# Decay attention and a squared-ReLU MLP on one core: maxima of the unsplit heads three slots sooner, and one pair of heads divided on 64 replicated rows of sums

## The chip, the cores and the metric

The kernel runs on one core of a Trainium2 chip. The metric is the device time of one execution in microseconds (us). A profiled execution has a span, from its first to its last instruction, and a time of its own, which is a little longer. Engines are named as in the profile: PE is TensorE's matmul side and PEld its weight loads, DVE is VectorE, ACT is ScalarE, POOL is GpSimd, SP is SyncE, which issues most DMAs.

## The reference

Eight batches of eight heads, 576 positions, head dimension 64; then an MLP over the 4608 tokens.

```
def _attn_ref(q, k, v, f):
    scores = scale * np.matmul(q, k.transpose(0, 1, 3, 2))
    log_f = np.log(np.clip(f, 0.0001, 1.0))
    cum = np.cumsum(log_f, axis=-1)
    decay = cum[:, :, :, None] - cum[:, :, None, :]
    scores = np.where(causal, -1000000000.0, scores + decay)
    scores = scores - np.max(scores, axis=-1, keepdims=True)
    attn = np.exp(scores)
    attn = attn / (np.sum(attn, axis=-1, keepdims=True) + 1e-09)
    return np.matmul(attn, v)

def _moe_ref(x, w_in, w_out):
    h = np.maximum(x @ w_in, 0.0)
    return h * h @ w_out
```

The MLP takes x with all heads of a token side by side (512 wide), w_in is 512 x 2048 and w_out 2048 x 512.

## The kernel before, in words

**Slots.** The 64 heads are cut into slots, six to a head (`UNITS`): slot n = 6h + u is unit u of head h, a block of keys against the queries that may see it. The main loop goes over n from -12 to the end and writes out one slot's instructions at a time; `in_order` then keeps each engine in that order. Per slot come: the scores of (h, u) (`score`, L342 and L344, then the exponential on ACT, L361), the product of probabilities and v of two slots earlier (`av_part`, L408; `LAG` is 2), parts of the division (`finish`), the events planned for the slot's two halves with `at`, weight steps (`cv`), and MLP work (`fill`).

**Whole and split heads.** The first 14 heads (`NWHOLE`) run scores and products in full fp32 from the tile `whole[h % 2]` (named rl in the profile). The rest run as sums of rounded products, with more work on DVE and POOL. The opening, up to slot 84, is the unsplit part; there the MLP's weights are also loaded and split.

**Maxima.** The exponential needs each query's maximum first. `max_units(h)` makes six small units from a rounded copy of q and k (`rounded[h % 2]`, rk in the profile, loaded by POOL): a matmul (L309) and a reduction on DVE (L315) that writes a column of `tcol`. Each of the last reductions of the five query blocks is followed by a DMA on SP (L321) that turns the column into a piece of row 66 of the head's operand. The scores of head h read that row. For an unsplit head the units stand in slots 0, 0.5, 1, 1.5, 2, 2.5 of the head ahead (`MAXIMA`). The query blocks are done from the last to the first. Maxima have two PSUM banks in turn (`banks["m"]`: 4 and 5), scores three, until the MLP begins.

**Division.** Each v tile carries a column of ones, so that row 64 of the product is the sum of probabilities; ACT copies 64 rows to `xt` (L422) and the row of sums to `den` (L423). For each pair of heads `finish` has four parts: two DMAs spread the sums over 128 partitions as 128 x 9 (`cmp`, L433); DVE adds 1e-9 and takes reciprocals (L435, L436), and a DMA writes them to DRAM (`rdr`, L438); two DMAs broadcast them to 64 rows each (L441); POOL multiplies `xt` by them (L444). For the first batch the parts stand 2, 5, 8 and 11 slots after the pair's last slot (`DIVIDE`).

**MLP.** Tokens go in chunks of 256 over 16 blocks of the hidden layer: 16 steps a chunk, each of two halves, `mlp1` (L474, then ACT and DVE) and `mlp2` (L497) a step later. `fill` spreads the halves evenly between `ready[b-1]` and `ready[b]`, where `ready[b]` is two slots after batch b's last division: 60 for the first batch, 104 for the second. `split_x` (L461, L462) makes the MLP's rounded operand from `xt`; for the first batch it stands two slots ahead of `ready[0]`. When the first chunk's step lacks weights, the next chunk is begun, and scores then have two banks (`banks.update`).

**Weights.** 32 tiles, each in five steps: four on DVE (L189, L194, L199, L201, with a magnitude on ACT, L178, a step ahead), then a cast on ACT (L206) and a subtraction on POOL (L207). Tiles are loaded up to four ahead (L169). `RATES` says how many steps a slot takes in five stretches: n below -6, below -3, below 0, up to `ready[0]`, and after.

Of the kernel before, what the change touches and what calls it, by code (L numbers as in the profile page):

```python
# [9 lines left out]
F32 = mybir.dt.float32  # L10
# [26 lines left out]
def decay_attention_relu2_kernel(  # L37
# [18 lines left out]
    nc = tc.nc  # L56

    NH, D, _, S = qk.shape
    P = 2 * D
    H = 8  # L60
    B = NH // H
    NJ = v.shape[2]
    NT, DM = out.shape
    NF = w_in.shape[0]
    NCC = DM // P
    T = 256
# [4 lines left out]
    EPS = 1e-9  # L71
# [4 lines left out]
    NWHOLE = 14  # L76
    DEPTH = 4
    cpool = ctx.enter_context(tc.tile_pool(name="cpool", bufs=1))
    wk = ctx.enter_context(tc.tile_pool(name="wk", bufs=2))
# [5 lines left out]
    def bank(use):  # L85

        turn = banks[use] or banks["s"]
        b = turn.pop(0)
        turn.append(b)
        return psum.tile([P, 512], F32, name=f"bank{b}")  # L90
# [21 lines left out]
    whole = [wk.tile([P, 2, S], F32, name="rl") for _ in range(2)]  # L112
# [23 lines left out]
    def load_f():  # L136
        nc.sync.dma_start(out=ft, in_=f)
# [84 lines left out]
    QT = [(0, D)] + [(D + i * P, P) for i in range((S - D) // P)]  # L222
# [4 lines left out]
    NU = len(UNITS)  # L227
    state = {}
# [8 lines left out]
    def load_cum(h, k):  # L237

        if h < 2:
            nc.sync.dma_start(out=f32(k[D:D + 2, :]), in_=cum[0][h:h + 1])  # L240
        else:
            nc.sync.dma_start(out=f32(k[D:D + 2, :]), in_=cum_dr[h])
# [9 lines left out]
    def load_whole(h):  # L252
# [3 lines left out]
        if cum:  # L256
            load_cum(h, x[:, 1])

    def load_v(h):
        if h < NH:  # L260
            vr = state[h]["vr"] = wk.tile([P, NJ, D + 2], F32, name="v", bufs=3)
            nc.sync.dma_start(out=vr[:, :, :D], in_=v[h])
            if h < NWHOLE:
                nc.gpsimd.memset(vr[:, :, D:], 1.0)
# [34 lines left out]
    def max_units(h):  # L299

        st = state[h]
        tcol = wk.tile([P, 8], F32, name="tcol")

        def unit(i, k0, n, init, last):
            q0, m = QT[i]
            end = q0 + m
            ps = bank("m")
            rows = P if h < NWHOLE else D + 2
            nc.tensor.matmul(  # L309
                ps[:m, :n], st["r2"][:rows, q0:q0 + m], st["kl0"][:rows, k0:k0 + n],  # L310
                start=True, stop=True,
            )
            mo = MW - P + (k0 if m < P else max(P - end + k0, P - MW))
            acc = tcol[:m, i:i + 1] if last else tcol[:m, 7:8]
            nc.vector.tensor_tensor_reduce(  # L315
                out=ps[:m, :n], in0=ps[:m, :n], in1=mz[:m, mo:mo + n],
                op0=ALU.add, op1=ALU.min, scale=-1.0, scalar=init, accum_out=acc,
            )
            if last:
                r = st["whole"][:, 0] if h < NWHOLE else st["r2"].bitcast(F32)  # L320
                nc.sync.dma_start(out=r[D + 2:D + 3, q0:end], in_=acc)  # L321

        us = []
        for i, (q0, m) in reversed(list(enumerate(QT))):
            end = q0 + m
            if end <= 512:
                us.append(lambda i=i, end=end: unit(i, 0, end, 1e30, True))
            else:
                us.append(lambda i=i: unit(i, 0, QA, 1e30, False))
                us.append(lambda i=i, end=end: unit(i, QA, end - QA, tcol[:, 7:8], True))  # L330
        return us

    def score(h, u):
        st = state[h]
# [47 lines left out]
    def av_split(st, acc, u, o, i, first, last):  # L382
        j = UNITS[u][0]
        ph, pl = st["p"][u]
        vh, vl = st["vh"][:, j, :D + 1], st["vl"][:, j, :]
        nc.tensor.matmul(acc[:D + 1, o], vh, pl[:, i], start=first, stop=False)  # L386
        nc.tensor.matmul(acc[:D, o], vl, ph[:, i], start=False, stop=False)  # L387
        nc.tensor.matmul(acc[:D + 1, o], vh, ph[:, i], start=False, stop=last)  # L388

    def av_part(h, u, low):  # L390

        j, q0, q1 = UNITS[u]
        s0, s1 = (q0, min(q1, QA)) if low else (max(q0, QA), q1)
        if s0 >= s1:
            return
        st = state[h]
        first = u == (NU - 1 if low else 0)
        last = u == NU - 2
        if first:
            st["av"] = bank("av")  # L400
        acc = st["av"]
        base = 0 if low else QA
        o, i = slice(s0 - base, s1 - base), slice(s0 - q0, s1 - q0)
        if h < NWHOLE:

            vr = st["vr"].rearrange("p j d -> p (j d)")
            vr = vr[:, j * (D + 2):min(j * (D + 2) + P, NJ * (D + 2))]
            nc.tensor.matmul(acc[:vr.shape[1], o], vr, st["p"][u][:, i], start=first, stop=last)  # L408
        else:
            av_split(st, acc, u, o, i, first, last)  # L410
        if last:
            n = QA if low else S - QA
            if not low:
                if h % H == 0:
                    xts[h // H] = wk.tile([P, NCC, S], F32, name=f"xt{h // H % 2}", bufs=1)
                if h % 2 == 0:
                    st["den"] = wk.tile([P, S], F32, name="den")
                else:
                    st["den"] = state[h - 1]["den"]
            o = (h % 2) * D  # L420
            x = xts[h // H][o:o + D, (h % H) // 2, base:base + n]
            nc.scalar.copy(out=x, in_=acc[:D, :n])  # L422
            nc.scalar.copy(out=st["den"][o:o + 1, base:base + n], in_=acc[D:D + 1, :n])  # L423

    def finish(h, part):

        st = state[h]
        den = st["den"]
        if part == 0:
            st["cmp"] = wk.tile([P, S // D], F32, name="cmp")  # L430

            for i in range(2):
                nc.sync.dma_start(out=st["cmp"][i * D:(i + 1) * D], in_=den[i * D:i * D + 1, :])  # L433
        if part == 1:
            nc.vector.tensor_scalar_add(st["cmp"], st["cmp"], EPS)  # L435
            nc.vector.reciprocal(out=st["cmp"], in_=st["cmp"])  # L436
            st["rdr"] = dr.tile([2, S], F32, name="rdr")
            nc.sync.dma_start(out=st["rdr"].rearrange("h (p c) -> (h p) c", p=D), in_=st["cmp"])  # L438
        if part == 2:
            for i in range(2):  # L440
                nc.sync.dma_start(out=den[i * D:(i + 1) * D], in_=st["rdr"][i:i + 1].broadcast_to([D, S]))  # L441
        if part == 3:
            x = xts[h // H][:, (h % H) // 2, :]
            nc.gpsimd.tensor_tensor(out=x, in0=x, in1=den, op=ALU.mult)  # L444
            del state[h], state[h - 1]
# [98 lines left out]

    RATES = (1, 0.5, 1.5, 1.4, 2.5)
    LAG = 2
    NA = H * NU


    DIVIDE = (2, 5, 8, 11), (2, 4, 6, 7)
    MAXIMA = (0, 0.5, 1, 1.5, 2, 2.5), (1.5, 2, 2.5, 3, 3.5, 4)
    SPLIT = 0, 1, 1, 3
    LOAD = 4
    VLOAD, VSPLIT = 2, 4
# [7 lines left out]

    def fin(h, part):

        return (h + 1) * NU - 1 + DIVIDE[h >= H][part]

    avs = {}
    for n, (h, u) in enumerate(slots):  # L570
        avs.setdefault(n + LAG, []).append((h, u))
    fins = {}
    for h in range(1, NH, 2):
        for part in range(4):
            fins.setdefault(fin(h, part), []).append((h, part))
    last_slot = max(fins)
    ready = [fin(b * H + H - 1, 3) + 2 for b in range(B)]

    def fill(n, part):
# [22 lines left out]
    def cv(k):  # L602
        owed[0] += k
        convert(int(owed[0]))
        owed[0] -= int(owed[0])
# [3 lines left out]
    def at(n, half, do, *args):  # L609
        events.setdefault((n, half), []).append(lambda: do(*args))  # L610

    def max_unit(h, i):
        if i == 0:
            state[h]["max"] = max_units(h)
        state[h]["max"][i]()

    for h in range(NH):
        split = h >= NWHOLE
        if split:
            at((h - 2) * NU + LOAD, 0, load, h)  # L620
            for part in range(4):
                at((h - 1) * NU + SPLIT[part], 1, prep, h, part)
        else:
            if h > 1:
                at((h - 3) * NU + 3, 0, load_rounded, h)
                at((h - 2) * NU + 5, 1, load_whole, h)
        at((h - 1) * NU + VLOAD, 1, load_v, h)
        at((h - 1) * NU + VSPLIT, 1, split_v, h)
        for i, x in enumerate(MAXIMA[split]):
            at((h - 1) * NU + int(x), int(2 * x) % 2, max_unit, h, i)  # L630
    for b in range(B):
        at(ready[b] - 2, 0, split_x, b * S // T, b + 1)
    load_f()
    load_rounded(0)
    convert(1)
# [22 lines left out]
    for n in range(-2 * NU, last_slot + 1):  # L658
# [4 lines left out]
        if live:  # L663
            h, u = slots[n]
# [11 lines left out]
        for do in events.get((n, 0), ()):  # L676
            do()
        wr = RATES[0 if n < -NU else 1 if n < -NU // 2 else 2 if n < 0 else 3 if n < ready[0] else 4]
        cv(wr / 2)
# [50 lines left out]
```

## Time and profile before

| | |
|---|---|
| time, median of 3 runs | 1240.69 us (1238.24 to 1242.15) |
| profiled execution, its own time | 1240.77 us |
| its span | 1239.0 us |
| PE busy | 1183.2 us, 95% |
| PEld busy | 1049.6 us, 85% |
| DVE busy | 785.4 us, 63% |
| ACT busy | 701.0 us, 57% |
| POOL busy | 382.5 us, 31% |

The page's second part cuts the span into 40 equal slices and gives each engine's busy share in tenths; PEclk is the clock that TensorE was granted. A list of waits gives engine, line and tile, who was waited for, then the total in us, the number of waits and the longest. A table by stretches gives the stretch, its length, the busy us of PE, PEld, DVE, ACT and POOL with counts of instructions, the granted clock, the busy share of the DMA engines, and GB/s. A timeline gives start, duration, engine, line, operation, tiles and shapes, and in brackets the idle time before it and what ended that. Groups by shape give total busy us, mean ns, and idle time before. A wait for several semaphores is put down to the one that came last by the profile.

### The profile page before, as it was taken

What the parts mean: (1) busy time and instruction counts of PE and PEld (TensorE: products, weight loads), DVE (VectorE), ACT (ScalarE), POOL (GpSimd) and SP (SyncE); (2) the same over time, 40 slices, a digit from 0 to 9 for tenths busy, and PEclk for the clock granted to TensorE, in tenths of its full rate; (3) what the DMA queues carried; (4) which work ended last, traced back from release to release, by engine and by line L of the source; (5) the groups of instructions that cost most, each with busy time, mean ns of one, the idle gap of its engine ahead of it and who ended that gap; (6) DMA issues with size and microseconds to landing.
All of it is one profiled execution on the core that took longest, in us unless ns stands there. A gap on an engine that the chain in (4) does not pass through costs nothing.

```text
span 1239.0 us, 23289 instructions
## 1 busy us (share of the span) xinstructions
PE 1183.2 (95%) x7652; PEld 1049.6 (85%) x7652; DVE 785.4 (63%) x2044; ACT 701.0 (57%) x1720; POOL 382.5 (31%) x574
## 2 busy tenths in 40 slices
PE   3887999999999999999999999999999999999998
PEld 2555787888999899989999989998999899999997
DVE  7666677767676767666656666677676767533322
ACT  2655455566666666665565666666666666632332
POOL 3333224433333433323223233334333333200000
PEclk9989899999999999999999999999999999999999
DMA  7767640212121111121202121211121222000000
GB/s 189 172 165 179 151 125 16 53 31 58 41 58 41 48 36 49 41 58 26 58 17 53 32 58 41 52 34 47 41 58 41 58 41 58 11 28 1 18 18 17
DMA packets 115440, 71.91 MB, mean 58 GB/s; under 512 B 97244, under 2 KB 97244, under 8 KB 115320
## 3 DMA queue, kind: packets, MB, share of 16 engines
q1 hardware_dynamic: 114200, 66.30, 21.9%
q0 software_dynamic: 1120, 4.13, 1.4%
q8 instruction: 61, 1.00, 0.3%
q14 instruction: 59, 0.48, 0.1%
HBM read 60.19 MB, written 9.88 MB: 57 GB/s over the span
## 4 chain that ended last, share of the span: by engine, by line
PE 53%; ACT 2%; issue 1%; POOL 1%; DMA 1%; DVE 0%; SPq 0%; POOLq 0%; DVEq 0%; ACTq 0%
PE bank L474 21%; PE bank L497 21%; PE bank L386 2%; PE bank L351 2%; PE bank L309 2%; PE bank L388 2%; PE bank L387 2%; PE bank L348 2%; DMA den<-rdr 1%; ACT r L482 0%; ACT ph L376 0%; ACT den L423 0%; ACT p L361 0%; POOL xt L444 0%; ACT rl L277 0%
## 5 line engine op out<-in xcount | busy, mean ns | idle before, releaser
L497 PE MATMUL bank<-w,gh 128*128 128x512 f32 x1152 | 412.9, 399 | 0.0
L474 PE MATMUL bank<-xh,w 128*128 128x256 f32 x2304 | 330.7, 286 | 2.2 <-DVE tcol L315 2.1
L377 DVE TENSOR_TENSOR pl<-p,ph 128x320 fp32r<-128x320 f32 (+4 forms) x300 | 189.7, 632 | 195.3 <-ACT ph L376 187.0
L474 PEld LDWEIGHTS bank<-xh,w 128*128 128x128 f32 x2304 | 302.3, 190 | 10.2 <-DVE tcol L315 2.7
L497 PEld LDWEIGHTS bank<-w,gh 128*128 128x128 f32 x1152 | 217.1, 188 | 38.2
L482 ACT ACTIVATE r<-bank 128x256 f32<-128x256 f32 x288 | 110.6, 384 | 206.7 <-PE bank L474 193.7
L497 PE MATMUL bank<-w,gl 128*128 128x512 f32 x576 | 226.6, 393 | 0.2 <-DVE gl L485 0.2
L483 DVE TENSOR_TENSOR g<-r 128x256 f32<-128x256 f32 x288 | 127.6, 443 | 141.1 <-ACT r L482 140.3
L363 POOL TENSOR_SCALAR_AFFINE_SELECT p<-p 128x128 f32<-128x128 f32 (+1 forms) x250 | 81.6, 326 | 421.3 <-ACT p L361 267.4
L376 ACT CAST ph<-p 128x320 fp32r<-128x320 f32 (+4 forms) x300 | 124.4, 415 | 148.9 <-POOL p L363 147.1
L474 PE MATMUL bank<-xl,w 128*128 128x256 f32 x1152 | 185.5, 283 | 0.0
L474 PEld LDWEIGHTS bank<-xl,w 128*128 128x128 f32 x1152 | 158.9, 191 | 0.0
L315 DVE CUSTOM_DVE_ANT_0 bank<-bank,mz 128x256 f32<-128x256 f32 (+4 forms) x320 | 133.8, 432 | 36.6 <-PE bank L309 33.1
L361 ACT ACTIVATE p<-bank 128x320 f32<-128x320 f32 (+4 forms) x300 | 116.0, 387 | 63.9 <-PE bank L351 51.8
L485 DVE TENSOR_TENSOR gl<-g,gh 128x256 fp32r<-128x256 f32 x288 | 127.8, 444 | 36.1 <-ACT p L361 1.0
L309 PE MATMUL bank<-rk 66*128 66x320 f32 (+9 forms) x384 | 113.8, 322 | 25.1 <-DVE tcol L315 10.8
L484 ACT ACTIVATE gh<-r 128x256 fp32r<-128x256 f32 x288 | 120.5, 419 | 9.1
L497 PEld LDWEIGHTS bank<-w,gl 128*128 128x128 f32 x576 | 109.1, 189 | 14.2 <-DVE gl L485 0.9
L309 PEld LDWEIGHTS bank<-rk 66*128 66x128 f32 (+3 forms) x384 | 69.4, 186 | 43.1 <-DVE tcol L315 20.4
L386 PE MATMUL bank<-pl,vh 128*65 128x320 f32 (+4 forms) x350 | 97.1, 278 | 2.3 <-ACT den L423 2.3
L387 PE MATMUL bank<-ph,v 128*64 128x320 f32 (+4 forms) x350 | 95.0, 271 | 0.0
L388 PE MATMUL bank<-ph,vh 128*65 128x320 f32 (+4 forms) x350 | 93.3, 272 | 0.0
(75 smaller groups left out, 1515.3 us busy)
## 6 DMA issues: line engine op xcount, KB each, us to landing
qkraw<-in_qk SPq DMA_DIRECT2D x50, 288.0 KB
v<-in_v SPq DMA_DIRECT2D x64, 160.0 KB
den<-rdr SPq DMA_DIRECT2D x64, 144.0 KB
out<-osb SPq DMA_DIRECT2D x36, 256.0 KB
w<-in_w_in SPq DMA_DIRECT2D x16, 512.0 KB
w<-in_w_out SPq DMA_DIRECT2D x16, 512.0 KB
rk<-in_qk POOLq DMA_DIRECT2D x14, 288.0 KB, 4.2
rl<-in_qk SPq DMA_DIRECT2D x14, 288.0 KB
```

Source lines behind the costliest of these rows:

```text
L309: nc.tensor.matmul(ps[:m, :n], st["r2"][:rows, q0:q0 + m], st["kl0"][:rows, k0:k0 + n], start=True, stop=True,)
L315: nc.vector.tensor_tensor_reduce(out=ps[:m, :n], in0=ps[:m, :n], in1=mz[:m, mo:mo + n], op0=ALU.add, op1=ALU.min, scale=-1.0, scalar=init, ...
L376: nc.scalar.copy(out=ph[:, :n], in_=p[:, :n])
L377: nc.vector.tensor_tensor(out=pl[:, :n], in0=p[:, :n], in1=ph[:, :n].bitcast(F32), op=ALU.subtract,)
L386: nc.tensor.matmul(acc[:D + 1, o], vh, pl[:, i], start=first, stop=False)
L387: nc.tensor.matmul(acc[:D, o], vl, ph[:, i], start=False, stop=False)
L388: nc.tensor.matmul(acc[:D + 1, o], vh, ph[:, i], start=False, stop=last)
L474: nc.tensor.matmul(ph[:, :T], w[:, s, cc], x[:, cc, :], start=(cc == 0 and k == 0), stop=(cc == NCC - 1 and k == 2),)
L483: nc.vector.tensor_tensor(out=g, in0=r, in1=r, op=ALU.mult)
L484: nc.scalar.activation(out=gh, in_=r, func=AF.Square)
L485: nc.vector.tensor_tensor(out=gl, in0=g, in1=gh.bitcast(F32), op=ALU.subtract)
L497: nc.tensor.matmul(po, g[:, ts], w[:, s], start=(fc == 0 and k == 0), stop=(fc == NF - 1 and k == 2),)
```

## The change

Five things:

- The maxima of unsplit heads are planned three slots sooner, in slots -3 to -0.5 of the head ahead (`MAXIMA`). The rounded copy of q and k two heads on is loaded three slots sooner too.
- The DMAs of an unsplit head's maxima leave the units and go together, all five, in the second half of slot 0 of the head ahead (`max_rows`).
- The last pair of the first batch (heads 6 and 7, `replicated`) has 64 columns of ones beside each block of v, in tiles whose names are those of the last two weight tiles. The sums then come out on 64 partitions, ACT copies 64 rows of them to `den`, DVE adds and takes reciprocals on the whole of `den`, and POOL multiplies. There are no DMAs. The two parts stand 3 and 4 slots after the pair's last slot (`DIRECT`), so that `ready[0]` is 53.
- The first `split_x` stands one slot ahead of `ready[0]`.
- Weight steps per slot: 1 instead of 1.4 up to `ready[0]`, then 2.8 instead of 2.5.

```diff
+    def replicated(h):
+        return h // 2 == H // 2 - 1
+
     def load_v(h):
-        if h < NH:
+        if replicated(h):
+            vr = wk.tile([P, 2 * DM], F32, name=f"w{2 * NF - 1 - h % 2}", bufs=1)
+            vr = state[h]["vr"] = vr[:, :NJ * P].rearrange("p (j d) -> p j d", d=P)
+            nc.sync.dma_start(out=vr[:, :, :D], in_=v[h])
+            nc.gpsimd.memset(vr[:, :, D:], 1.0)
+        elif h < NH:
...
-            if last:
-                r = st["whole"][:, 0] if h < NWHOLE else st["r2"].bitcast(F32)
-                nc.sync.dma_start(out=r[D + 2:D + 3, q0:end], in_=acc)
+            if last and h >= NWHOLE:
+                nc.sync.dma_start(out=st["r2"].bitcast(F32)[D + 2:D + 3, q0:end], in_=acc)
...
+    def max_rows(h):
+        st = state[h]
+        r = st["whole"][D + 2:D + 3, 0]
+        for i, (q0, m) in reversed(list(enumerate(QT))):
+            nc.sync.dma_start(out=r[:, q0:q0 + m], in_=st["tcol"][:m, i:i + 1])
...
-            vr = vr[:, j * (D + 2):min(j * (D + 2) + P, NJ * (D + 2))]
+            d = st["vr"].shape[2]
+            vr = vr[:, j * d:min(j * d + P, NJ * d)]
...
-            nc.scalar.copy(out=st["den"][o:o + 1, base:base + n], in_=acc[D:D + 1, :n])
+            m = D if replicated(h) else 1
+            nc.scalar.copy(out=st["den"][o:o + m, base:base + n], in_=acc[D:D + m, :n])
...
+        if part == 1 and replicated(h):
+            nc.vector.tensor_scalar_add(den, den, EPS)
+            nc.vector.reciprocal(out=den, in_=den)
+            return
...
-    RATES = (1, 0.5, 1.5, 1.4, 2.5)
+    RATES = (1, 0.5, 1.5, 1, 2.8)
...
-    MAXIMA = (0, 0.5, 1, 1.5, 2, 2.5), (1.5, 2, 2.5, 3, 3.5, 4)
+    DIRECT = {1: 3, 3: 4}
+    MAXIMA = (-3, -2.5, -2, -1.5, -1, -0.5), (1.5, 2, 2.5, 3, 3.5, 4)
...
-        return (h + 1) * NU - 1 + DIVIDE[h >= H][part]
+        return (h + 1) * NU - 1 + (DIRECT if replicated(h) else DIVIDE[h >= H])[part]
...
-                at((h - 3) * NU + 3, 0, load_rounded, h)
+                at((h - 3) * NU, 0, load_rounded, h)
                 at((h - 2) * NU + 5, 1, load_whole, h)
+            at((h - 1) * NU, 1, max_rows, h)
...
-        at(ready[b] - 2, 0, split_x, b * S // T, b + 1)
+        at(ready[b] - 1 - (b > 0), 0, split_x, b * S // T, b + 1)
```

More of the change, by code (lines that the diff above doesn't have):

```diff
@@ L301, in max_units @@
         st = state[h]
-        tcol = wk.tile([P, 8], F32, name="tcol")
+        tcol = st["tcol"] = wk.tile([P, 8], F32, name="tcol")
         def unit(i, k0, n, init, last):
@@ L573, in decay_attention_relu2_kernel @@
     for h in range(1, NH, 2):
-        for part in range(4):
+        for part in DIRECT if replicated(h) else range(4):
             fins.setdefault(fin(h, part), []).append((h, part))
@@ L629, in decay_attention_relu2_kernel @@
         for i, x in enumerate(MAXIMA[split]):
-            at((h - 1) * NU + int(x), int(2 * x) % 2, max_unit, h, i)
+            at((h - 1) * NU + math.floor(x), int(2 * x) % 2, max_unit, h, i)
     for b in range(B):
-        at(ready[b] - 2, 0, split_x, b * S // T, b + 1)
+        at(ready[b] - 1 - (b > 0), 0, split_x, b * S // T, b + 1)
     load_f()
```

## The prediction

> **What bounds the kernel now.** I read the page's 40 slices first, then the waits of the first 130 us, then busy times by head, then the timeline around one wait, then VectorE's groups by shape.
>
> ```profile
> PE   3887999999999999999999999999999999999998
> PEclk9989899999999999999999999999999999999999
> ```
>
> A slice is 31 us. After the fourth, TensorE is the limit for the rest of the run: what the change saves must be idle or slow-clock time of TensorE in the opening. Its total work does not change (the same matmuls, in another order), so I sum losses, not work.
>
> ```profile
> PE bank L342 <- DMA rl<-tcol: 13.7, 7, 3.9
> ACT wmag L178 <- DMA w<-in_w_out: 12.9, 2, 6.9
> PE bank L342 <- DMA v<-in_v: 3.7, 1, 3.7
> ```
>
> The longest of TensorE's waits that recurs: the scores (L342) wait for rows of maxima that a DMA turns from `tcol` into the head's `whole` tile. The 3.7 us put down to v is of the same kind, as the timeline below shows.
>
> Now by head. Head h's first score is in slot 6h; each stretch runs from that matmul to the next head's. They are heads 1 to 9, then 10 and 11:
>
> ```profile
> 32.94:40.81 7.87, 7.17 (x40) 5.21 (x39) 5.71 (x18) 5.07 (x13) 2.20 (x4) 1.00 0.68 171
> 40.81:51.45 10.64, 7.63 (x41) 5.26 (x39) 7.03 (x21) 6.79 (x16) 3.58 (x6) 1.00 0.84 193
> 51.45:60.84 9.39, 7.57 (x38) 5.29 (x38) 7.21 (x19) 5.45 (x13) 3.68 (x6) 1.00 0.64 152
> 60.84:69.51 8.67, 7.36 (x37) 5.28 (x38) 5.44 (x17) 5.60 (x13) 4.18 (x6) 1.00 0.92 214
> 69.51:81.44 11.93, 7.83 (x37) 5.27 (x38) 8.56 (x23) 5.72 (x14) 4.28 (x7) 0.96 0.79 192
> 81.44:92.31 10.87, 10.26 (x38) 7.11 (x38) 6.17 (x20) 5.04 (x12) 2.56 (x5) 0.74 0.38 109
> 92.31:103.63 11.32, 7.36 (x39) 5.28 (x38) 8.02 (x21) 6.58 (x16) 4.49 (x7) 1.00 0.95 205
> 103.63:113.53 9.90, 9.20 (x37) 6.31 (x38) 6.60 (x20) 4.59 (x11) 3.12 (x5) 0.83 0.52 143
> 113.53:124.60 11.07, 7.73 (x38) 5.28 (x38) 6.29 (x18) 6.22 (x15) 3.95 (x6) 1.00 0.84 190
> 124.60:149.16 24.56, 22.44 (x116) 18.45 (x117) 16.86 (x40) 10.35 (x24) 5.79 (x7) 0.79 0.61 143
> 149.16:168.91 19.75, 19.75 (x118) 16.48 (x117) 14.85 (x34) 11.13 (x27) 5.80 (x6) 1.00 0.71 210
> ```
>
> The first number is the length, then busy PE, PEld, DVE, ACT, POOL, the granted clock, DMA share, GB/s. At clock 1.00 a head is some 7.45 us of TensorE (7.17 to 7.73). The nine heads take 91.66 us, so 91.66 - 9 x 7.45 = 24.6 us are lost. Rows account for about 15.4 (13.7 + 3.7, less 2.0 before 32.94 us). Slow clock behind waits of over 3 us accounts for some 4.6 (10.26 and 9.20 against 7.45). The other 4.6 us, 0.5 a head, are short waits.
>
> Why rows come late, at head 6:
>
> ```profile
> 76.05 0.13 DVE L315 DVE_READ_ACCUMULATOR2_ANT tcol<- 64x1 f32 x1
> 76.22 1.83 SPq L321 DMA_DIRECT2D rl<-tcol  x3
> 78.14 0.60 SPq L262 DMA_DIRECT2D v<-in_v  x1
> 78.84 0.85 SPq L321 DMA_DIRECT2D rl<-tcol  x1
> 81.44 1.41 PE L342 MATMUL bank<-rl 128*128 128x320 f32 x2 [3.65 <-DMA v<-in_v]
> ```
>
> By plan the maxima end in slot 2.5 of the head ahead. That head began at 69.51, and VectorE finished at 76.05: 6.5 us in, where 2.5 slots of 7.45/6 = 1.24 us are 3.1. Then SP issues three row requests from 76.22 to 78.05, and the score starts 3.4 us after the last of these: some 4 us of latency for the rows that the first score reads (its columns begin at 256, so it needs the first three of five).
>
> **The change, part by part.** *Maxima sooner, rows together.* Maxima are planned three slots sooner; the five requests follow in slot 0.5 of the head ahead. TensorE can be only two maxima ahead of VectorE (two banks), so VectorE is done about 1 us after slot 0; requests follow at 1.83/3 = 0.6 us each. The third leaves at 0.7 + 1.0 + 1.8 = 3.5 us, lands at 7.5, and a head without row waits lasts 7.45 + 0.5 = 7.95. So it is just in time, with 0.45 us to spare, and a busy DMA queue will still make some late. I take 0.35 us a head for that, so 8.3 us a head; ends: 0 (7.95) and 1.1 (9.05, if latency is 5.5 us). On SP, v, weight loads and the sums of the pair now stand behind five requests that wait for VectorE: weights are staged four tiles ahead, v two heads of buffers, so I cost that at nothing; if the cover fails, ScalarE waits for a tile as it did for 6.9 us in the waits above. Loading q and k three slots sooner keeps its distance to its use (nine slots); its issue on POOL and its cumulative row on SP wait for TensorE half a slot back, as before.
>
> *Rates.* From slot 0, 1 weight step a slot, not 1.4; five steps are a tile, so 1.2 tiles a head, not 1.68. Cost of a tile:
>
> ```profile
> L199 DVE SCALAR_TENSOR_TENSOR osb<-w,osb 128x512 int32<-128x512 int32 x19 | 15.1, 796 | 0.3
> L201 DVE SCALAR_TENSOR_TENSOR osb<-w,osb 128x512 int32<-128x512 int32 x19 | 13.9, 732 | 0.3
> L189 DVE TENSOR_SCALAR wmag<-wmag 128x512 f32<-128x512 f32 x20 | 13.3, 664 | 5.1 <-ACT wmag L178 5.1
> L194 DVE TENSOR_SCALAR osb<-wmag 128x512 int32<-128x512 int32 x19 | 12.0, 633 | 0.7
> L435 DVE TENSOR_SCALAR cmp<-cmp 128x9 f32<-128x9 f32 x4 | 1.4, 359 | 2.7 <-DMA cmp<-den 2.7
> L462 DVE TENSOR_TENSOR xl<-xt,xh 128x1024 fp32r<-128x1024 f32 x1 | 1.2, 1226 | 0.0
> L436 DVE RECIPROCAL cmp<-cmp 128x9 f32<-128x9 f32 x4 | 0.9, 216 | 0.1
> L461 DVE CAST xh<-xt 128x1024 fp32r<-128x1024 f32 x1 | 0.7, 695 | 4.2 <-POOL xt L444 4.2
> ```
>
> That is 0.80 + 0.73 + 0.66 + 0.63 = 2.8 us of VectorE a tile, 1.3 us a head less, and 245 KB of traffic:
>
> ```profile
> w<-in_w_in SPq DMA_DIRECT2D x12, 512.0 KB
> rk<-in_qk POOLq DMA_DIRECT2D x13, 288.0 KB, 4.2
> rl<-in_qk SPq DMA_DIRECT2D x12, 288.0 KB
> v<-in_v SPq DMA_DIRECT2D x11, 160.0 KB
> ```
>
> A head's own loads are 736 KB, so 1.35 MB a head for 1.60. VectorE's mean of the nine heads, 6.8 us, falls to some 5.4 of 8.3: neither binds here. In before, slot 60 comes 54 slots after slot 6, the nine heads; in after, the MLP may start at slot 53, 47 slots or 7.83 heads on. Loss: 7.83 x (8.3 - 7.45) = 6.7 us, where 24.6 were lost. Gain 17.9.
>
> *The opening.* Head 1's maxima now stand ahead of the first score. The fourth weight tile, for which ScalarE waits (the 6.9 us), is requested behind four more maxima, some 2 us of VectorE; TensorE has by slot 6 done about 1 us of head 2's maxima that before still owed. Net loss 1 (ends 0 and 4).
>
> *The last pair.* Sums come out of the same matmul on 64 rows. The copies cost the same:
>
> ```profile
> 34.27 0.42 ACT L422 COPY xt<-bank 64x320 f32<-64x320 f32 x1
> 34.70 0.42 ACT L423 COPY den<-bank 1x320 f32<-1x320 f32 x1
> ```
>
> Five DMAs and their latency go. In their place VectorE adds and takes reciprocals of 128x576. No row shows that. [...] I take the step from an undisturbed add of the same 9 to the reciprocal,
>
> ```profile
> 90.33 0.16 DVE L435 TENSOR_SCALAR cmp<-cmp 128x9 f32<-128x9 f32 x1
> ```
>
> which is 0.06/9 = 6.7 ns an element, so 3.9 us for 576, and 0.6 for the add and start: 4.5 us for both. [...]
>
> How the junction goes now:
>
> ```profile
> 119.69 1.27 POOL L207 TENSOR_TENSOR w<-osb,w 128x512 fp32r<-128x512 f32 x1 [4.06 <-ACT w L206]
> 119.80 1.49 DVE L194 TENSOR_SCALAR osb<-wmag 128x512 int32<-128x512 int32 x1
> ...
> 124.11 1.39 POOL L444 TENSOR_TENSOR xt<-xt,den 128x576 f32<-128x576 f32 x1 [1.75 <-DMA den<-rdr]
> ...
> 129.26 2.08 PE L474 MATMUL bank<-xh,w 128*128 128x256 f32 x8 [2.12 <-DVE tcol L315]
> ```
>
> Slot 50's division holds VectorE; head 10's maxima (slots 51 to 53.5), queued behind it, keep their banks, and TensorE stops at slot 52 for the third. After the division come POOL's product (1.39), the split of x (0.70 + 1.23) and the first MLP matmul. From the last sums at slot 49 that is 1.2 + 4.5 + 1.4 + 0.7 = 7.8 us and some 2 us of maxima and weight steps between, against four slots or 5 us of TensorE's own work: 5 us idle, and 2.5 of slow clock behind it (2.8 and 1.75 in the rows above), 7.5 in all. The same junction now loses 24.56 - 19.7 = 4.9. Net loss 2.6 (ends 0 and 12).
>
> *Slots 53 to 104.* The same 64 MLP halves are spread over 51 slots, not 44. A slot of head 11 is 19.75/6 = 3.3 us, 2.05 of that for 1.45 halves; with 1.25 halves it is 3.0. Weights cost VectorE 0.06 x 2.8 more a slot, the thinner MLP less, so its 14.85/6 = 2.5 us stay: 83% where it was 75%. Chunk 1, which leaves the scores two banks, starts near slot 71, not 80. I take 3 us for both (ends 0 and 10).
>
> Sum: 17.9 - 1 - 2.6 - 3 = 11.3 us. The profiled execution took 1240.77 us (span 1239.0), 0.08 above the median: 1229.5.
>
> **Rivals.** *More:* rows never late (loss 3.9), junction as before, opening free, VectorE no hindrance: 24.6 - 3.9 = 20.7, so 1220. For it: heads 1 and 4 run in 7.87 and 8.67 now.
>
> *Rows late anyway:* the first request leaves no sooner than before, and shorter heads ask for the same 736 KB in less time. At 9.3 us a head the loss is 14.5, and the gain 24.6 - 14.5 - 6.6 = 3.5: 1237; at 9.6, 1239.6. For it: DMA shares of 0.92 and 0.95; against: both those heads carried more weight tiles than will come.
>
> *VectorE binds from slot 53 on:* the rate of 2.8 meets a shorter slot. L194 took 1.49 us beside POOL's subtraction at 119.8, for 0.63 in the mean. If L189 and L194 were stretched so each time, by a further 0.9, VectorE would need 2.5 + 0.56 x 2 x 0.9 = 3.5 us of a 3.0 us slot for the 34 slots of weights: 17 us, less the 3 taken: 1243.5; with the larger junction, 1250. It decides against the change from 3.4 us a slot. Against it: head 11 shows 75%.
>
> **Chances.** Forecast 0.57 (1224 to 1236), more 0.16, rows late 0.17, VectorE 0.10. The range leaves out the slow case and the tail of the best: 1218 to 1240. A measurement can tell about 0.3%, 3.7 us. Faster takes the forecast nearly whole, more, and a few of rows late: 0.76; same 0.14; slower 0.10.
>
> **What would show it.** Waits of L342 for rows under 4 us in all; heads 2 to 7 at 8.0 to 8.7 us, clock near 1.00; reciprocals of 128x576 at 3.3 to 5.5 us, a gap of TensorE right behind slot 51; the first MLP matmul near 108 us, not 129.26; DVE under 90% for the 75 us after it. Wrong if heads stay above 9.3 us, if the gap is over 10, or if L474 and L497 wait for VectorE.

## The result and the profile after

The changed kernel takes 1246.82 us in the median of 11 runs (1242.78 to 1250.7); the kernel before, in runs beside it, 1239.29 (1236.52 to 1245.87). The ratio is 1.0057, with a 95% interval of 1.0037 to 1.0077: slower by some 7 us where 11 us of gain were forecast. The profiled execution has a span of 1244.2 us, for 1239.0 before.

The page of the changed kernel, its slices of 31 us; the first four digits are about those of before (3887), and the clock dips in the fourth slice where it dipped in the third and the fifth:

```profile
PE   4887998899999999999999999999999999999998
PEclk9998999899999999999999999999999999999999
```

The new 8s are the seventh and eighth digits, 187 to 249 us, where before had 9. TensorE's waits over the whole run (its engine and line, who was waited for, total, number, longest):

```profile
PE bank L319 <- DVE tcol L325: 22.0, 15, 3.6
PE bank L319 <- DMA rk<-qkraw: 9.9, 1, 9.9
PE bank L319 <- DVE rk L286: 3.5, 4, 1.7
```

The waits of scores for rows, 13.7 + 3.7 us in before, are gone from the list. The first line is that of the maxima's matmuls (L309 before, L319 now), which wait until VectorE has read a bank: 22.0 us, of which 16.3 lie in the first 130 us; before had 6.7 there by its own trace. One wait has in part taken the place of the other.

By head, from head 1's first score to the first MLP matmuls, the same table as in the prediction (length, then busy PE, PEld, DVE, ACT, POOL, clock, DMA share, GB/s):

```profile
32.71:40.42 7.71, 7.62 (x38) 5.21 (x38) 4.98 (x19) 4.27 (x11) 2.43 (x4) 1.00 0.74 174
40.42:51.65 11.23, 7.67 (x39) 5.22 (x38) 5.17 (x20) 5.68 (x14) 2.04 (x4) 1.00 0.66 155
51.65:61.21 9.56, 9.35 (x38) 6.20 (x38) 5.06 (x18) 4.87 (x12) 2.69 (x5) 0.82 0.76 182
61.21:70.53 9.32, 7.88 (x38) 5.21 (x38) 7.50 (x20) 5.50 (x13) 4.08 (x6) 1.00 0.62 138
70.53:78.24 7.71, 7.62 (x38) 5.22 (x38) 5.01 (x18) 4.77 (x12) 2.62 (x4) 1.00 0.70 142
78.24:88.47 10.23, 7.81 (x39) 5.32 (x38) 6.57 (x21) 4.53 (x12) 3.96 (x5) 1.00 0.67 174
88.47:96.19 7.72, 7.63 (x38) 5.31 (x38) 4.81 (x17) 5.62 (x14) 2.02 (x4) 1.00 0.75 186
96.19:114.61 18.42, 11.62 (x50) 8.42 (x50) 12.92 (x24) 5.60 (x13) 6.29 (x7) 0.79 0.65 131
```

Heads 1, 5 and 7 run in 7.7 us, as a head without waits should. Heads 2, 4 and 6, in which the sums of the pair before are divided, take 9.3 to 11.2, and a clock of 0.82 makes head 3 long as well. The last stretch is the junction with the MLP. The timeline around the longest wait of head 2:

```profile
46.30 0.42 DVE L194 TENSOR_SCALAR osb<-wmag 128x512 int32<-128x512 int32 x1
...
49.93 0.17 DVE L457 TENSOR_SCALAR cmp<-cmp 128x9 f32<-128x9 f32 x1 [3.20 <-DMA cmp<-den]
50.14 0.22 DVE L458 RECIPROCAL cmp<-cmp 128x9 f32<-128x9 f32 x1
50.27 0.61 DVE L325 CUSTOM_DVE_ANT_0 bank<-bank,mz 128x448 f32<-128x448 f32 x1
...
50.99 0.69 PE L319 MATMUL bank<-rk 128*128 128x192 f32 x2 [3.47 <-DVE tcol L325]
```

VectorE stood for 3.2 us in front of the add on the sums, whose DMA had not landed. Behind it in VectorE's queue stood a maximum; TensorE, with both banks full, stopped for 3.5 us. By plan this add (part 1 of the division) is in slot 4 of every second head. The maxima of before were in slots 0 to 2.5 and done by then; moved three slots, they are in slots 3 to 5.5 of the head before their old place, around it.

The junction, where VectorE divides the sums of heads 6 and 7:

```profile
100.29 1.78 DVE L448 TENSOR_SCALAR den<-den 128x576 f32<-128x576 f32 x1 [2.44 <-ACT den L441]
100.44 1.28 POOL L207 TENSOR_TENSOR w<-osb,w 128x512 fp32r<-128x512 f32 x1
...
102.11 3.75 DVE L449 RECIPROCAL den<-den 128x576 f32<-128x576 f32 x1
...
106.04 1.42 POOL L466 TENSOR_TENSOR xt<-xt,den 128x576 f32<-128x576 f32 x1 [3.87 <-DVE den L449]
...
106.60 0.48 PE L319 MATMUL bank<-rk 128*128 128x448 f32 x1 [3.64 <-DVE tcol L325]
...
111.82 2.08 PE L496 MATMUL bank<-xh,w 128*128 128x256 f32 x8 [2.37 <-DVE tcol L325]
```

The reciprocal takes 3.75 us, the add 1.78 beside POOL's subtraction. TensorE stops for 3.64 us behind the second maximum of head 10, and for 2.37 before the first MLP matmul; the clock of the stretch is 0.79.

To see where time goes between kernels I use the exponentials (one a slot, in order): the time of slot 48, when no MLP has begun in any of them, and of slot 102, when each has done 31 MLP steps. From slot 48 to 102 the work of TensorE is so the same in all, but for a few matmuls. Before reaches slot 48 at 104.5 us and slot 102 at 269.2; the changed kernel at 97.1 and 275.3. So it leads by 7.5 us at slot 48 and trails by 6.1 at slot 102. Both are single executions: the changed kernel and four below that are like it up to slot 48 (`after_r34`, `after_light`, `after_norecip`, `after_light_norecip`) reach it at 97.1 to 100.6 us, so a lead there is good to 3 or 4 us.

### The profile page after: what moved, and what is told of

Read it like the earlier page. It is cut to its first block, busy times and chain, and to the rows that moved or that the text cites. A ratio compares the mean times of both kernels' runs of the same rounds, so it can differ in the third digit from the quotient of the medians.

```text
span 1244.2 us, 23243 instructions
## 1 busy us (share of the span) xinstructions
PE 1189.3 (96%) x7652; PEld 1050.2 (84%) x7652; DVE 786.7 (63%) x2044; ACT 699.5 (56%) x1720; POOL 380.9 (31%) x574
## 5 line engine op out<-in xcount | busy, mean ns | idle before, releaser
L496 PEld LDWEIGHTS bank<-xh,w 128*128 128x128 f32 x2304 | 303.2, 191 | 11.2 <-DVE tcol L325 2.6
L505 DVE TENSOR_TENSOR g<-r 128x256 f32<-128x256 f32 x288 | 131.2, 455 | 143.2 <-ACT r L504 142.6
L319 PE MATMUL bank<-rk 66*128 66x320 f32 (+9 forms) x384 | 113.7, 322 | 39.4 <-DVE tcol L325 22.0
L319 PEld LDWEIGHTS bank<-rk 66*128 66x128 f32 (+3 forms) x384 | 69.4, 186 | 56.8 <-DVE tcol L325 29.7
```

Source lines behind the costliest of these rows:

```text
L319: nc.tensor.matmul(ps[:m, :n], st["r2"][:rows, q0:q0 + m], st["kl0"][:rows, k0:k0 + n], start=True, stop=True,)
L496: nc.tensor.matmul(ph[:, :T], w[:, s, cc], x[:, cc, :], start=(cc == 0 and k == 0), stop=(cc == NCC - 1 and k == 2),)
L505: nc.vector.tensor_tensor(out=g, in0=r, in1=r, op=ALU.mult)
```

## The experiments

The theories. **A**: the sooner maxima stand behind VectorE's wait for the sums' DMA. **B**, later in the texts **T** and **V**: weight steps are a fixed amount; put off from the early heads, where TensorE idled, to slots after 53, they cost there. **R**: the long reciprocal is the loss. **D**: the DMA engines are too full in the early heads for any order to help. The tables of slots stand at the end of the section.

### The three parts one by one, and two at a time

`m_only` has the sooner maxima alone, `r_only` the last pair's division, `t_only` the rates; `mt`, `mr` and `rt` have two of the three. The edits undo parts of the change:

```diff
-    RATES = (1, 0.5, 1.5, 1, 2.8)
+    RATES = (1, 0.5, 1.5, 1.4, 2.5)          # no T
...
-        return h // 2 == H // 2 - 1
+        return False                            # no R, and the first split_x at ready - 2
...
-    MAXIMA = (-3, -2.5, -2, -1.5, -1, -0.5), (1.5, 2, 2.5, 3, 3.5, 4)
+    MAXIMA = (0, 0.5, 1, 1.5, 2, 2.5), (1.5, 2, 2.5, 3, 3.5, 4)   # no M, rows and loads as before
```

> Only the maxima three slots sooner, with their rows together and the rounded copies loaded sooner; rates and the division of the last pair as before. Theory A (order on VectorE: the maxima now stand behind the add on the sums, which waits for its DMA, every second head, and the long reciprocal): without the reciprocal the gain of the early heads is kept, about 7 us by slot 48, less 1 to 3 us at the divisions of heads 9, 11 and 13: 1232 to 1236 us, and heads still alternate between about 8 and 11 us. Theory B (the loss comes with the other rates and the earlier MLP): same numbers up to slot 60 and nothing lost after it, 1230 to 1233 us. If the sooner maxima themselves are at fault: 1240 us or more.

Measured: 1238.55 us, ratio 1.0007 (0.9987 to 1.0026). No gain. TensorE's waits in slots of the early heads (30 to 105 us):

```profile
PE bank L319 <- DVE tcol L325: 11.0, 11, 2.3
PE bank L358 <- DMA v<-in_v: 0.9, 1, 0.9
```

12.1 us of waits for rows in that stretch of before (8.4 and 3.7) have become 11.0 on VectorE, for 2.6 in before. Neither theory had that: I had given the sooner maxima the 7 us that only came with the slower rates.

> Only the last pair's division on VectorE by sums on 64 partitions, with the MLP from slot 53; maxima and rates as before. Theory A: the reciprocal of 3.75 us stands in front of no maxima of its own stage except those at slot 54, the junction costs about what it costs before, the early start gains little: 1238 to 1241 us. Theory B: the MLP spread over 51 slots costs what slots 53 to 104 lost in the changed kernel: 1243 to 1247 us.

Measured: 1240.87 us, 1.0025 (1.0008 to 1.0042). The upper end of A's range: the early MLP is no gain, and no great loss.

> Only the other rates, 1 and 2.8 weight steps a slot; maxima and division as before, MLP from slot 60. Theory A: heads a little shorter, by 0.3 us each, the weights done at slot 92: 1237 to 1241 us. Theory B: the weight steps pushed into the MLP stage bind VectorE there: 1243 to 1247 us.

Measured: 1253.76 us, 1.0137 (1.0107 to 1.0167), more than B expected. By slot 48 it leads by 2.7 us, by slot 102 it trails by 13.

> The change without the last pair's division on VectorE: maxima sooner and the other rates, MLP from slot 60. Theory A: the junction's long stop goes (some 5 us), the alternation of the heads stays: 1236 to 1240 us. Theory B: no better than the changed kernel: 1243 to 1247 us.

Measured: 1250.94 us, 1.011 (1.0084 to 1.0137): B, and worse than the changed kernel. The MLP and the faster second rate begin later there (slot 60), and the weights are done near slot 92, not 87; that this is the reason is likely, but no run separates the two.

> The change with the rates of before (1.4 and 2.5): sooner maxima, last pair's division on VectorE. Theory T (the slower early weights run on into the split heads, where VectorE already has the splits of the probabilities; that is where the time is lost): the loss of slots 78 to 102, 11 us in the changed kernel, goes, and so does the gain of 7.5 us by slot 48, which the sooner maxima alone did not have: 1239 to 1243 us. Theory R (the last pair's division and its long reciprocal is the loss): 1246 us as the changed kernel.

Measured: 1243.68 us, 1.0041 (1.0021 to 1.006). Just above theory T's range. The lead at slot 48 goes (107.7 us), and so does the loss behind it. By its time it can't be told from the changed kernel, as the intervals overlap: with the other two parts in place, the rates bring ahead of slot 48 about what they cost behind it.

> The last pair's division and the other rates, with the maxima of before. Putting off 4.2 tiles costs 12 to 14 us after slot 48, the early heads gain 2 to 3 us as the rates alone did: 1247 to 1252 us, slower than the changed kernel. If instead the sooner maxima harm (by standing behind the long reciprocal): 1240 to 1244 us, faster than the changed kernel.

Measured: 1251.33 us, 1.0107 (1.0082 to 1.0132): as the first case. Without the sooner maxima the change is worse. The 2 to 3 us at the early heads did not come: slot 48 is reached at 104.9 us, before at 104.5.

### Where the put-off weight steps cost

The stretch from slot 84 to 102, in which the split heads give VectorE and POOL more to do: first before (13 MLP steps), then the changed kernel (11), `r_only` (11) and `t_only` (13):

```profile
211.20:269.17 57.97, 54.97 (x355) 49.18 (x354) 40.35 (x102) 33.69 (x86) 23.20 (x32) 0.97 0.19 48
```

```profile
214.04:275.28 61.24, 53.31 (x316) 45.34 (x315) 39.28 (x100) 32.77 (x83) 23.47 (x33) 0.92 0.18 44
```

```profile
218.36:269.98 51.62, 47.25 (x314) 41.75 (x313) 32.28 (x91) 30.95 (x79) 18.60 (x28) 1.00 0.19 48
```

```profile
211.29:282.22 70.93, 56.02 (x340) 48.63 (x339) 49.63 (x111) 37.46 (x92) 25.97 (x34) 0.93 0.13 34
```

For the same work the changed kernel needs 9.6 us more than `r_only`, whose weights are done at slot 83 by the same count that gives 87 for the change; VectorE is busy for 7 us more, POOL for 5. `t_only`, with weights until slot 92, needs 13 us more than before. Does it help to finish the weights ahead of slot 84?

```diff
-    RATES = (1, 0.5, 1.5, 1, 2.8)
+    RATES = (1, 0.5, 1.5, 1, 3.4)
```

> The change with 3.4 weight steps a slot from slot 53 on instead of 2.8, so that the weights are done near slot 81, ahead of the split heads (slot 84). Theory T: slots 78 to 102 take 6 to 10 us less: 1237 to 1241 us. Rival (weight steps cost VectorE and so TensorE the same wherever they stand after slot 53): 1245 to 1248 us, the loss moved to slots 54 to 78.

Measured: 1246.2 us, 1.0072 (1.0047 to 1.0097). The rival. The two stretches 54 to 84 and 84 to 102, of this kernel and of the changed one:

```profile
117.88:225.26 107.38, 93.73 (x516) 74.18 (x514) 85.60 (x173) 55.53 (x129) 35.64 (x36) 0.97 0.35 100
225.26:274.99 49.73, 46.88 (x313) 41.61 (x313) 30.41 (x88) 30.10 (x77) 18.53 (x28) 1.00 0.21 51
```

```profile
116.06:214.04 97.98, 92.06 (x520) 74.45 (x520) 76.87 (x166) 53.40 (x124) 30.21 (x32) 0.98 0.43 118
214.04:275.28 61.24, 53.31 (x316) 45.34 (x315) 39.28 (x100) 32.77 (x83) 23.47 (x33) 0.92 0.18 44
```

The last stretch is 11.5 us shorter, the one ahead of it 9.4 longer (with nearly the same MLP work): the price moved with the steps. It is of the same order per tile in every pair of kernels that differ in the rates alone. From slot 48 to 102: `t_only` 180.4 for 164.7 in before, `mt` 181.4 for 164.6 in `m_only`, both with 24 steps or 4.8 tiles left over at slot 60, so 3.3 and 3.5 us a tile; `rt` 178.7 for 164.6 in `r_only`, the change 178.2 and `after_r34` 176.4 for 166.0 in `mr`, with 21 steps or 4.2 tiles at slot 53: 3.4, 2.9 and 2.5. Each pair changes both rates, but 2.8 and 3.4 steps a slot cost about the same; so it is the steps put off that cost, not the speed at which they are made up.

In what form does TensorE pay? Where the MLP begins at slot 60, it waits for VectorE. From slot 54 to 102, first before, then `t_only`:

```profile
PE bank L309 <- DVE tcol L315: 3.1, 3, 2.2
```

```profile
PE bank L319 <- DVE tcol L325: 11.6, 7, 3.8
```

All its waits there that end with VectorE come to 5.7 and 17.5 us, which is nearly the whole idle time that `t_only` has more (in `m_only` and `mt` to 5.8 and 18.4). In the changed kernel they come to 6.4, and in `mr` to 5.7. Slots 48 to 102 of `mr`, then of the changed kernel:

```profile
107.72:273.76 166.04, 148.99 (x884) 123.24 (x883) 118.25 (x270) 87.49 (x214) 55.84 (x68) 0.98 0.32 87
```

```profile
97.06:275.28 178.22, 157.57 (x884) 128.62 (x883) 128.96 (x285) 92.57 (x221) 60.57 (x73) 0.93 0.36 93
```

Of the 12.2 us between them 8.6 are a longer busy time for the same matmuls, at a clock of 0.93 for 0.98, and 3.6 are idle time. So the put-off steps cost the changed kernel mainly slow clock; what brings that on is not shown.

Is it VectorE's part of a tile? Two of its four instructions are left out on tiles 13 to 31, in the change and in before:

```diff
-            nc.vector.scalar_tensor_tensor(wi, high, -0x40000000, wi, ...)
+            if i < 13: nc.vector.scalar_tensor_tensor(wi, high, -0x40000000, wi, ...)
...
-            nc.vector.scalar_tensor_tensor(wi, low, 29, wi, ...)
+            if i < 13: nc.vector.scalar_tensor_tensor(wi, low, 29, wi, ...)
```

> The changed kernel, where the weight tiles from the 14th on leave out two of VectorE's four instructions (the merges of their words, 1.5 us a tile, so those weights are not the reference's). Theory V (the change puts weight work, a fixed amount, from slots where TensorE idled to slots 53 to 102, where VectorE holds TensorE up; 4.2 tiles of 2.8 us): 19 tiles x 1.5 = 29 us less of VectorE there, slots 48 to 102 shorter by 12 to 20 us: 1226 to 1236 us, and no longer behind the kernel before with the same omission. Rival (the thinner MLP, or two banks for the scores from slot 71 on, is what costs): 1243 us or more.

> The kernel before with the same omission (two of VectorE's four instructions on the weight tiles from the 14th on). Theory V: it gains less than the changed kernel, since its TensorE waits for rows in the early heads and not for VectorE, and its later slots are less full: 1230 to 1237 us. Rival: unchanged, 1239 us, and still 5 us or more ahead of the changed kernel with the same omission.

Measured: 1240.93 us, 1.002 (1.0002 to 1.0038), and 1236.39, 0.9989 (0.9968 to 1.0009). Before gains nothing that can be told, though its time lies in V's range; the change gains 0.37%, between theory and rival, and stays 0.3% behind its counterpart, which V had not. From slot 48 to 102 the omission gives the change 7.8 us and before 3.1. So VectorE's work there costs the change, as V says, but not alone: what is left out is half of VectorE's share of a tile, and its reciprocal stands as before.

The rival does not carry the rest. By the order that the kernels write out, chunk 1, and with it the two banks, begins at slot 74 in `after_r34` and in `mr` alike, and both spread the MLP from slot 53; yet they differ by 10.4 us from slot 48 to 102.

> The changed kernel without the add and the reciprocal on the sums of heads 6 and 7 (those two heads of the first batch stay multiplied by their sums). Theory V: 5.5 us of VectorE and the stop of TensorE at slot 52 go: first MLP matmul 4 to 6 us sooner, 1239 to 1242 us. Rival (the junction's loss is hidden by the VectorE bound that follows or comes from the product on GpSimd): 1245 us or more.

The edit is `return` in the place of the add and the reciprocal. Measured: 1242.46 us, 1.0025 (1.0007 to 1.0043): theory V, 0.5 us past the end of its range: 0.3%, about 4 us for 5.5 us of VectorE.

> The changed kernel with both omissions: two of VectorE's four instructions on weight tiles from the 14th on, and the add and reciprocal on the sums of heads 6 and 7. If the two terms are separate and add up, about 4.5 and 6 us: 1235 to 1238 us. If they are one (VectorE full from slot 50 on, either omission fills the same hole): 1239 to 1241 us.

Measured: 1235.97 us, 0.9975 (0.9959 to 0.9991). The two terms add up (0.37 + 0.32%, and 0.82% together, within the intervals): with both gone the change is ahead of before, though not clearly of `before_light`. That version leaves work out; it shows the size of the terms and is no gain.

### Why the sooner maxima alone bring nothing

First, the add and reciprocal put behind the maxima, two slots later, with the rest of the division (all unsplit pairs but the last of the first batch):

```diff
+    DIVIDE = (2, 5, 8, 11), (2, 4, 6, 7), (2, 7, 10, 13)     # the third for h < NWHOLE
```

> The change with the add and reciprocal on the sums of unsplit pairs, which wait for a DMA, planned two to four slots later, behind the maxima of their head instead of among them. Theory A (order on VectorE): the heads that take 9.3 to 11.2 us come down to some 8, slot 48 is reached 5 to 9 us sooner, 1237 to 1242 us. Rival (the alternation has another cause, the maxima are late for TensorE or DMA): no change, 1246 us.

Measured: 1245.63 us, 1.0061 (1.0039 to 1.0083). The rival: no gain, though the cause named by A is nearly out of the way (VectorE's waits for the sums fall from 5.8 to 1.6 us between slots 6 and 48). From 30 to 118 us the waits on VectorE that are left are mainly the junction's (3.4 and 2.4), and others stand in their place:

```profile
PE bank L319 <- DVE tcol L325: 3.4, 1, 3.4
PE bank L425 <- DMA v<-in_v: 2.6, 1, 2.6
PE bank L425 <- POOL pl L376: 2.5, 1, 2.5
PE bank L496 <- DVE tcol L325: 2.4, 1, 2.4
PE bank L358 <- DMA rl<-tcol: 2.3, 1, 2.3
```

POOL's product now waits for the broadcast (17.1 us in three waits, the longest 7.8), and what stands behind it on POOL, the clearing of a probability tile (L376), is late.

> Both: the later division and 3.4 steps a slot. If both theories hold and add up: 1229 to 1235 us. If either is wrong: 1237 us or more.

Measured: 1245.34 us, 1.0059 (1.0036 to 1.0083): not even both together.

> Sooner maxima alone, with the rates and the last pair of before, and the add and reciprocal of the other unsplit pairs behind the maxima, with four and five slots between the steps of their DMA round trip. Theory A plus V (no weight work put off, and VectorE no longer stopped among the maxima): heads 2 to 7 at 9 to 9.7 us instead of 10.4, 1232 to 1237 us. Rival (a wait of the round trip only moves to GpSimd's product or to v): 1238 to 1241 us.

With parts 2, 7, 11, 16 and the rates and last pair of before. Measured: 1242.37 us, 1.0028 (1.0009 to 1.0046). The rival, 1.4 us past its range: waits for v (4.8 us) and for rows (3.4) are back.

Then a third bank for the maxima (`"m": [4, 5, 7]`), so that TensorE can run ahead of VectorE by one more:

> Sooner maxima alone, with the rates and the division of before, and three PSUM banks for the maxima in place of two until the MLP begins. If TensorE stops because the third maximum needs a bank that VectorE, held up by the sums' DMA, has not read (theory A): its 11 us of waits on the maxima between slots 6 and 48 fall to 3 to 6 us, and the time to 1232 to 1236 us. If VectorE's amount of work sets the pace there (1.4 weight steps a slot and the maxima): the waits only move to the scores, which wait for rows, and the time stays at 1237 to 1240 us.

> The change with three banks for the maxima until the MLP begins. Theory A: the early waits (7 us) and part of the stop at slot 52 go, slot 48 comes 3 to 5 us sooner and the first MLP matmul too; 1241 to 1244 us. If VectorE sets the pace: 1246 us.

Measured: 1240.1 us, 1.0011 (0.999 to 1.0032), and 1246.84, 1.007 (1.0043 to 1.0097). No gain, near what was expected if VectorE sets the pace: from 30 to 118 us `m_3bank` has 4 waits on VectorE in place of 14 in `m_only`, but of up to 4.9 us, 14.1 in all for 14.8. VectorE itself is late (it waits 9.4 us for the sums, 5.2 in `m_only`); banks do not help.

Last, what makes VectorE late: its step on the sums left out (those heads are multiplied by their sums, not divided), or half of each weight tile's load left out (that half is set to zero by POOL).

```diff
-            nc.vector.tensor_scalar_add(st["cmp"], st["cmp"], EPS)      # m_nodiv: for h >= NWHOLE only
-            nc.vector.reciprocal(out=st["cmp"], in_=st["cmp"])
...
-                nc.sync.dma_start(out=raw, in_=...)                     # m_half
+                nc.sync.dma_start(out=raw[:, :DM], in_=...[:, :DM])
+                nc.gpsimd.memset(raw[:, DM:].bitcast(F32), 0.0)
```

> Sooner maxima alone, with VectorE's add and reciprocal on the sums of the unsplit pairs left out (the spread sums go out again as they are, so those heads are multiplied by their sums). If VectorE's stop for the sums' DMA is what holds the sooner maxima up (theory A): slot 48 some 5 to 8 us sooner than with the sooner maxima alone, 1230 to 1235 us. If the loaded DMA engines are what holds the early heads (theory D): no more than 2 us, 1237 to 1240 us.

> Sooner maxima alone, with half of each weight tile loaded, and the other half set to zero by GpSimd (so half of the weights are left out). Theory D: with 430 KB less a head the DMA share falls from 0.77 to some 0.6, the sums, v and rows land sooner, slot 48 comes 6 to 10 us sooner: 1227 to 1234 us. Theory A: the stop for the sums gets only a little shorter, 1235 to 1239 us.

Measured: `m_nodiv` 1238.2 us, 1.0006 (0.9991 to 1.0022); `m_half` 1232.37 us, 0.9952 (0.9934 to 0.9971). Both times lie in theory D's ranges; slot 48 comes 2.6 and 4.0 us sooner than in `m_only`, where D had at most 2, and 6 to 10. Without VectorE's step TensorE waits for v instead (30 to 118 us):

```profile
PE bank L425 <- DMA v<-in_v: 6.5, 2, 3.8
PE bank L319 <- DVE tcol L325: 4.6, 9, 0.7
```

With half the weight traffic, and POOL's extra work, the kernel with the sooner maxima is faster, and VectorE's wait for the sums falls from 5.2 us (`m_only`, 30 to 105 us) to 1.0. The DMA share from slot 6 to 48, first `m_only`, then `m_half`:

```profile
32.15:104.97 72.82, 60.32 (x261) 40.24 (x260) 46.66 (x138) 40.06 (x94) 24.50 (x36) 0.91 0.77 171
```

```profile
33.48:101.00 67.52, 58.12 (x263) 38.59 (x262) 48.58 (x138) 39.92 (x95) 31.29 (x49) 0.95 0.62 143
```

0.77 became 0.62, and the seven heads 5.3 us shorter. Before with half the traffic was not run, so how much of this needs the sooner maxima stays open.

### All kernels

| kernel | ratio to before | slot 48, us | slots 48 to 102, us |
|---|---|---|---|
| before | 1 | 104.5 | 164.7 |
| the change | 1.0057 | 97.1 | 178.2 |
| `m_only` | 1.0007 | 105.0 | 164.6 |
| `r_only` | 1.0025 | 105.4 | 164.6 |
| `t_only` | 1.0137 | 101.8 | 180.4 |
| `mt` | 1.011 | 96.7 | 181.4 |
| `mr` | 1.0041 | 107.7 | 166.0 |
| `rt` | 1.0107 | 104.9 | 178.7 |
| `after_r34` | 1.0072 | 98.6 | 176.4 |
| `after_late` | 1.0061 | 100.9 | 174.2 |
| `after_late_r34` | 1.0059 | 97.7 | 174.4 |
| `after_3bank` | 1.007 | 99.9 | 178.2 |
| `after_light` | 1.002 | 98.9 | 170.4 |
| `before_light` | 0.9989 | 101.4 | 161.6 |
| `after_norecip` | 1.0025 | 100.0 | 171.6 |
| `after_light_norecip` | 0.9975 | 100.6 | 164.3 |
| `m_late2` | 1.0028 | 102.1 | 166.3 |
| `m_3bank` | 1.0011 | 103.8 | 164.0 |
| `m_nodiv` | 1.0006 | 102.4 | 161.6 |
| `m_half` | 0.9952 | 101.0 | 162.4 |

No kernel that computes the whole of the reference is faster than before.

## Why the prediction was wrong

**Waits for rows.** Right that they go: from 17 us to none. Wrong that nothing would take their place. The prediction put the sums and the weights behind the five requests on SP and cost that at nothing; it never asked what the maxima themselves were moved past on VectorE. There the add on the sums stood in slot 4, with a DMA in front of it that it waited for, 3.20 us at head 2. I had 8.3 us a head; slots 6 to 48 gave 62.9/7 = 9.0, and 9.0 to 9.8 in the four kernels that are like it up to there. That is where the rival of late rows had the heads (9.3 to 9.6), though with another wait.

**The early gain.** Of the 17.9 us forecast, 12.6 fall to slots 6 to 48 (70.7 us in before, seven heads of 8.3 forecast). They gave 7.8 in the profiled execution, a lucky one: the mean of the five kernels alike up to there gives 5.2 (65.5 us for 70.7). It comes from the maxima and the slower rates together: kernels with both and no other edit that bears on it reach slot 48 at 96.7 to 100.6 us, with the maxima alone at 105.0 and 107.7 (`m_only`, `mr`), with the rates alone at 101.8 and 104.9 (`t_only`, `rt`), with neither at 104.5 and 105.4 (before, `r_only`). The prediction noted that 245 KB of traffic a head go and that DMA shares of 0.92 and 0.95 occur, but credited the whole gain to the order of the maxima. With the old weight traffic the wait moved from rows to the sums (5.2 us of VectorE in `m_only`) or to v (6.5 of TensorE in `m_nodiv`), with the slower rates in `after_late` to POOL's product (17.1 us on the broadcast); `m_half`, which takes away traffic and no work of VectorE, is faster (0.9952 for 1.0007 in `m_only`). The slower rates take away both, and no run says how much of their share is traffic.

**The step that failed most** is "slots 53 to 104": 3 us, with an end at 10. From slot 48 on the forecast comes to a loss of 0.3 us (17.9 - 12.6, less 2.6 for the junction and these 3); measured are 13.5 from slot 48 to 102. I worked out VectorE's load per slot, 83%, found it under 100, and stopped. What I left out is that a weight step not done in the early heads is still to be done: 21 steps, 4.2 tiles, moved out of slots in which TensorE stood anyway into slots in which it has work all the time. Each tile cost 2.5 to 3.5 us there; I had put that term at nothing. It is near the 2.8 us that the prediction itself had for VectorE's share of a tile, but the form is mixed: waits for VectorE in `t_only` and `mt`, in the changed kernel mainly a slower clock. The rival "VectorE binds" was nearest, with 17 us as its price, but I placed it in slots 53 to 87, by stretched instructions, and gave it 0.10. Its test, "DVE under 90% for the 75 us after it", held (76.87 of 97.98 us from slot 54 to 84 is 78%), and the time was lost all the same. In `t_only` the waits for VectorE rose by 11.8 us with VectorE busy 75% from slot 54 to 84 and 70% from 84 to 102: an average under 100% did not show that nobody waits.

**The junction.** The mechanism was right and the size not far off: 3.75 us for the reciprocal (forecast 3.9), but 1.78 for the add. The 0.6 that was forecast for it and the start was the author's estimate, which no row of before shows; the add took 0.46 us in `r_only`. TensorE stopped at the maxima behind it, 3.64 and 2.37 us, and the first MLP matmul came at 111.8 (108). `after_norecip` puts the two instructions at 0.3%, 4 us; the net 2.6 of the forecast was for the whole junction, which no run gives by itself (`r_only`, with the earlier MLP in it, is 0.25% slower than before).

**The opening.** Slot 6 came at 34.1 us for 33.8, a loss of 0.3 (forecast 1). The four kernels that are like it up to there came at 31.9 to 36.1, so that 0.3 and 1 can't be told apart.

**The sum.** The forecast's 12.6 to slot 48, less 1 for the opening and 0.3 behind slot 48, became in the profiled executions about 7.8 - 0.3 - 13.5, some 6 us of loss at slot 102; the spans at the end are 1244.2 us for 1239.0.

What is not settled: how much of a put-off tile's 3 us is VectorE's and how much POOL's and ScalarE's, and what brings on the slow clock. Half of VectorE's share left out gave back 7.8 us of the 13.5 between slots 48 and 102 (7.3 between `after_norecip` and `after_light_norecip`), and before gained 3.1 from the same omission. So about a third of the excess, 4.7 us, goes with VectorE's part, from single executions.

## What to carry to other kernels

Before moving a step sooner, list what stands around its new place on every engine it uses, not on the DMA queue alone: here an add waited 3.20 us for a DMA, the maximum behind it on VectorE waited with it, and TensorE stood for 3.47. Work that is slowed down in one stage comes back in another: ask for each put-off step whether the stage that receives it has idle time on the bounding engine, as the giving stage had. And when a wait vanishes and the time does not, look for what all the candidates share; here halving the weight loads gave 0.5%, where changes of order and banks gave nothing, though before was not run with the same halving.

## What the runs showed of the hardware

*The wait for the sums.* In `m_only` the add on the sums starts 1.8, 2.6 and 2.0 us after SP has issued the second of its two small DMAs (128 x 9 numbers in all), each time released by it. In `m_half`, with half the weight traffic, it starts 1.4 to 1.5 us after, so that the numbers had landed by then. VectorE's waits fell by more, from 5.2 to 1.0 us in all, because VectorE also came to the add later there, counted from the issue. The mean DMA share does not order these waits by itself: 5.2 us at 0.77 (`m_only`), 5.8 at 0.65 (`after_norecip`, slots 6 to 48), 1.0 at 0.62 (`m_half`).

*Slow clock.* The same matmuls took 157.6 us of TensorE in slots 48 to 102 at a clock of 0.93 (the change) and 149.0 at 0.98 (`mr`). In the changed kernel the clock was 1.00 ahead of the 3.47 us wait of head 2 (40.42 to 47.5 us), 0.82 from 51 to 53 us, 0.50 from 53 to 55, 0.82 from 55 to 57, and 1.00 again up to 61.21. By the table of heads, head 3's matmuls took 9.35 us there, for 7.62 in heads 1 and 5 at 1.00: some 1.7 us, an estimate from these two rows, on top of the wait. Whether the wait brings the slow clock on, no run tests.

*Add beside a subtraction.* The add on 128x576 took 1.78 us in the changed kernel, with POOL's subtraction on 128x512 in the same time, and 0.46 in `r_only`:

```profile
109.78 0.46 DVE L449 TENSOR_SCALAR den<-den 128x576 f32<-128x576 f32 x1
110.28 3.75 DVE L450 RECIPROCAL den<-den 128x576 f32<-128x576 f32 x1
```

The difference is 1.3 us, about the length of POOL's instruction, 1.28 us. What lengthens the add is not shown: by the profile it starts first in both kernels, 0.15 us ahead of POOL's subtraction in the changed one and 0.26 in `r_only`, where the subtraction took 1.33 us beside an add of 0.46.
